# Attention with top-k, then two gated MLPs, on one core: the sign of the weights coded in a scaling, and probabilities normalised before the transpose

## The chip, the cores and the metric

The kernel runs on one core of a Trainium2 chip. The metric is the device time in microseconds (us) of one execution. A core has a matrix engine (TensorE, PE in the profile; its weight loads are the rows PEld), a vector engine (VectorE, DVE), an activation engine (ScalarE, ACT), a general engine (GpSimd, POOL) and an engine that issues transfers (SyncE, SP). Each engine takes its own instructions in the order in which the program lists them.

## The reference

```python
scores = (q @ k.T) / sqrt(64)                       # 4 batches, 8 heads, 576 queries, 576 keys
kth    = np.partition(scores, -32, axis=-1)[..., -32:-31]
scores = np.where(scores >= kth, scores, -1e9)      # the 32 largest of a row stay
attn   = exp(scores - max); attn /= attn.sum(-1) + 1e-9
x = attn @ v                                        # 2304 tokens of 512 numbers
h = x @ w_in;  x = (h * sigmoid(h)) @ w_out         # 512 -> 2048 -> 512
h = (x @ w1) * (x @ w2)                             # 512 -> 1024
out = (h @ w3) @ w_out2                             # 1024 -> 1024 -> 512
```

The weights `w_in`, `w_out`, `w1`, `w2`, `w3` and `w_out2` (`w4` in the kernel) reach the core as 64-bit floating-point numbers, two 32-bit words for each, while q, k and v are 32-bit. The kernel has to make 32-bit numbers of the weights on the chip.

## The kernel before, in words

The 2304 tokens are cut into six blocks of 384 (three tiles of 128 queries). For each block there is an attention part (8 heads, 24 tiles of queries) and an MLP part. While the MLP of block j runs, the attention of block j+1 runs beside it; the attention of block 0 runs beside the conversion of `w3` and `w4` and their product (the "fold"). Almost every product in the MLPs is made of three passes over numbers that are split into a high and a low part.

**Attention of a tile.** PE makes the scores (L415, L416), ACT copies them out (L419), DVE finds the 32 largest in four passes of `max` (L446) with three of `match_replace` between them (L450). ACT masks and exponentiates (L466, L472), DVE takes the reciprocal of the row sum (`rc`, L481, L482), and `norm` (L484) applies it. PE then transposes 128 x 128 pieces of the probabilities (`tr` in `plan_av`), ACT copies these out (L564), and PE multiplies them with V (L584).

**Native blocks.** Blocks 0 and 1 (`NATIVE`) multiply with V in full 32-bit precision, without a split. In them `norm` does not touch the probabilities `e`: it scales the identity with `rc` into a diagonal `dg` (128 x 128), on ACT for the first four pairs of tiles (L496), on GpSimd after that (L498), and PE multiplies `e` with `dg` (L553), which transposes and normalises at once. Such a matmul of 32-bit numbers stands in the profile as two instructions, so the 240 of the program are x480. In blocks 2 to 5 GpSimd normalises `e` itself (128 x 640, L498), and PE transposes it with the identity (L556, L558), one instruction for each piece.

**Conversion of a piece of weights** (512 columns of 128 rows, 72 pieces: 24 in the fold, 48 for the other four matrices). `convert_load` fetches both words of each number. `convert_scale` scales the high word, read as a float, by 2^-112 into a tile `t`, which moves its exponent to where the 32-bit one belongs, and turns the low word into the bits that are missing (ACT, L140, with a bias from the tile `low`). `convert_bits` shifts `t` left by 3 and ORs the low bits in (DVE, L150). The shift loses the sign, and there are two ways to give it back. For even pieces outside the fold (24) ACT scales (L136) and a second DVE pass ORs the sign bit in (L153). For the other 48 GpSimd scales (L138), ACT makes a sign of +1 or -1 (L143) and GpSimd multiplies with it (L156). For the 48 pieces outside the fold the number is then split into a high part (ACT, L201) and a low part (GpSimd, L202) and written to memory, from where the later blocks read it. These 48 conversions run beside the last part of block 0's attention and beside the first MLP.

**What sets the order.** Attention work is put at ticks (`plan`), and the steps of an MLP, of the fold and of the conversion are spread over the ticks (`Spread`). The tile framework then orders the instructions of all engines by its own estimate of times, so a change in one instruction can move others far from it.

Of the kernel before, what the change touches and what calls it, by code (L numbers as in the profile page):

```python
# [8 lines left out]
FP32 = mybir.dt.float32  # L9
FP32R = mybir.dt.float32r  # L10
U32 = mybir.dt.uint32
I32 = mybir.dt.int32
ACTF = mybir.ActivationFunctionType
ALU = mybir.AluOpType
# [4 lines left out]
SHIFT = 2.0 ** -112  # L19
BLOCKS = [3, 3, 3, 3, 3, 3]  # L20
# [8 lines left out]
NORM_ACT = lambda n: n < 4  # L29
BELOW = 1.0e34  # L30
SLOT = 7
NATIVE = lambda j: j < 2
SCALE_ACT = lambda n, fold: not fold and n % 2 == 0
SIGN_BITS = lambda n, fold: not fold and n % 2 == 0
# [18 lines left out]
def attention_moe_moe2_kernel(  # L53
# [13 lines left out]
    nc = tc.nc  # L67
    B, H, D2, S = qT.shape
# [10 lines left out]
    scale = 1.0 / float(D) ** 0.5  # L79
# [10 lines left out]
    pt_p = ctx.enter_context(tc.tile_pool(name="pt", bufs=2))  # L90
# [25 lines left out]
    n_conv = [0]  # L116

# [9 lines left out]
    def convert_scale(r, fold):  # L130
        n = n_conv[0]
        n_conv[0] += 1
        t = raw_p.tile([128, 512], FP32, tag="t", bufs=TB, name="t")
        h = r[:, :, 1].bitcast(FP32)
        if SCALE_ACT(n, fold):
            nc.scalar.activation(out=t, in_=h, func=ACTF.Copy, scale=SHIFT)  # L136
        else:
            nc.gpsimd.tensor_scalar(t, h, SHIFT, 1.0, op0=ALU.mult, op1=ALU.mult)  # L138

        nc.scalar.activation(out=r[:, :, 0].bitcast(I32), in_=r[:, :, 0], func=ACTF.Identity,  # L140
                             bias=low, scale=2.0 ** -29 * (1.0 - 2.0 ** -16))
        if not SIGN_BITS(n, fold):
            nc.scalar.activation(out=h, in_=h, func=ACTF.Sign)  # L143
        return t, SIGN_BITS(n, fold)

    def convert_bits(r, t_):
        t, bits = t_
        w = raw_p.tile([128, 512], FP32, tag="w", bufs=WB, name="w")
        wb, tb = w.bitcast(U32), t.bitcast(U32)
        nc.vector.scalar_tensor_tensor(out=wb, in0=tb, scalar=3, in1=r[:, :, 0],  # L150
                                       op0=ALU.logical_shift_left, op1=ALU.bitwise_or)
        if bits:
            nc.vector.scalar_tensor_tensor(out=wb, in0=r[:, :, 1], scalar=0x80000000, in1=wb,  # L153
                                           op0=ALU.bitwise_and, op1=ALU.bitwise_or)
        else:
            nc.gpsimd.tensor_tensor(out=w, in0=w, in1=r[:, :, 1].bitcast(FP32), op=ALU.mult)  # L156
        return w
# [120 lines left out]
    blocks = []  # L278
# [149 lines left out]
    def plan_topk(n, base):  # L428
        pr = pairs[n]
        m = len(pr)  # L430
        st = {}
# [52 lines left out]
        def norm(i):  # L484
            j, h, t = pr[i]
            hd = heads[j, h]
            e = st["e"][i]

            if NATIVE(j):
                if "d" not in hd:  # L490
                    hd["d"] = pt_p.tile([128, blocks[j][1]], FP32, tag="pl", bufs=3, name="dg")
                x, p = ident, hd["d"][:, t * 128:(t + 1) * 128]
            else:
                x = p = e
            if NORM_ACT(n):
                nc.scalar.activation(out=p, in_=x, func=ACTF.Copy, scale=st["rc"][:, i:i + 1])  # L496
            else:
                nc.gpsimd.tensor_scalar(p, x, st["rc"][:, i:i + 1], 1.0, op0=ALU.mult, op1=ALU.mult)  # L498
            hd["p"][t] = e
            tiles.pop(n, None)  # L500
# [20 lines left out]
    def plan_av(j, h):  # L521
# [12 lines left out]
        def begin():  # L534
            st["p"] = heads[j, h]["p"]
            st["d"] = heads[j, h].get("d")
# [7 lines left out]
        for kc in range(KC):  # L544
            u = {}

            def tr(u=u, kc=kc):
                u["ps"] = ps = bank("pt")
                for i in range(BLOCKS[j]):
                    p = st["p"][i]  # L550
                    if native:
                        kn = REM if kc == NFULL else 128
                        nc.tensor.matmul(ps[0:kn, i * 128:(i + 1) * 128], lhsT=p[:, kc * 128:kc * 128 + kn],  # L553
                                         rhs=st["d"][:, i * 128:(i + 1) * 128], start=True, stop=True)
# [346 lines left out]
```

## Time and profile before

| | us |
|---|---|
| three runs | 1194.24, 1195.57 (median), 1199.98 |
| profiled execution, its time | 1194.58 |
| its span (first to last instruction) | 1192.3 |
| MLP of block 0: first L655 to last L776 | 193.5 to 418.2 |
| last L776 of blocks 1 to 4 | 583.6, 746.8, 915.6, 1071.1 |

Times in the profile count from the start of the span. A row of a group of instructions reads: line, engine, operation, out<-in with shapes, count | busy us, mean ns of one | idle time of the engine just before them, and who ended it.

### The profile page before, as it was taken

The numbers are of one execution on the slowest core, as the hardware profiler recorded it, in microseconds if no ns is written. First come the engines' busy times: TensorE is split into PE (matmuls) and PEld (weight loads), VectorE is DVE, ScalarE is ACT, GpSimd is POOL, SyncE is SP. The second block draws the span as 40 slices with busy tenths as digits, with TensorE's granted clock in tenths as the row PEclk, the third lists the DMA queues.
The fourth block names the chain that finished last, engine by engine and source line by source line (L and its number), as shares of the span: only waits on it lengthen the run. The fifth ranks groups of instructions, "written<-read, shape, count | busy, mean of one in ns | idle before, by whom it ended". The sixth has DMA issues, their size and how long they took to land.

```text
span 1192.3 us, 19809 instructions
## 1 busy us (share of the span) xinstructions
PE 1117.7 (94%) x6216; PEld 989.3 (83%) x6216; DVE 933.7 (78%) x2136; ACT 860.6 (72%) x1931; POOL 760.5 (64%) x768
## 2 busy tenths in 40 slices
PE   4889959899889999999999999999999999999998
PEld 2445536788778899989899999999898999999997
DVE  6998899999999898988889897987789988701100
ACT  6786888798897587887778877877868778642221
POOL 5665583798987266686687866767755767542231
PEclk8899978999999999999999999999999999999999
DMA  9963484788979377757678776898766775538740
GB/s 296 296 212 111 144 303 162 242 283 322 344 271 338 109 230 249 226 186 231 216 226 279 234 245 206 294 314 274 253 205 212 235 241 171 187 113 281 244 166 26
DMA packets 127880, 273.54 MB, mean 229 GB/s; under 512 B 40480, under 2 KB 65056, under 8 KB 127776
## 3 DMA queue, kind: packets, MB, share of 16 engines
q1 hardware_dynamic: 119712, 245.02, 62.4%
q10 hardware_dynamic: 8064, 27.27, 5.9%
q8 instruction: 49, 0.80, 0.3%
q14 instruction: 55, 0.45, 0.1%
HBM read 216.14 MB, written 56.10 MB: 228 GB/s over the span
## 4 chain that ended last, share of the span: by engine, by line
PE 60%; ACT 6%; DVE 5%; issue 1%; POOL 1%; DMA 1%; SPq 0%; ACTq 0%; DVEq 0%
PE bank L656 13%; PE bank L657 13%; PE bank L655 13%; PE bank L776 8%; PE bank L593 4%; PE bank L556 3%; PE bank L415 2%; DVE top L446 2%; PE bank L416 2%; DVE wk L450 2%; DVE w L150 1%; ACT e L466 1%; PE bank L558 1%; ACT e L472 1%; PE bank L584 1%
## 5 line engine op out<-in xcount | busy, mean ns | idle before, releaser
L446 DVE MAX8 top<-wk 128x8 f32<-128x576 f32 x432 | 319.7, 752 | 3.7
L670 POOL TENSOR_TENSOR gl<-gf,gh 128x384 fp32r<-128x384 f32 x144 | 149.3, 1038 | 147.5 <-ACT gh L669 140.6
L450 DVE MATCH_REPLACE8 wk<-top,wk 128x576 f32<-128x576 f32 x288 | 213.3, 742 | 0.0
L574 POOL TENSOR_TENSOR pl<-pf,ph 128x384 fp32r<-128x384 f32 x128 | 129.7, 1020 | 66.3 <-ACT ph L572 57.6
L419 ACT ACTIVATE st<-bank 128x288 f32<-128x288 f32 (+1 forms) x320 | 127.7, 415 | 41.6 <-PE bank L416 39.1
L446 DVE MAX8 top<-st 128x8 f32<-128x576 f32 x144 | 107.6, 751 | 34.0 <-ACT st L419 33.7
L656 PE MATMUL bank<-gl,wt 128*128 128x384 f32 x384 | 131.6, 343 | 2.0 <-POOL gl L670 1.7
L655 PE MATMUL bank<-x2h,wt 128*128 128x384 f32 x384 | 131.6, 345 | 1.9 <-ACT x2h L714 1.4
L655 PE MATMUL bank<-xh,wt 128*128 128x384 f32 x384 | 130.4, 342 | 2.4 <-ACT pn L564 0.9
L656 PE MATMUL bank<-x2l,wt 128*128 128x384 f32 x384 | 130.2, 339 | 2.2 <-POOL x2l L715 1.9
L656 PE MATMUL bank<-xl,wt 128*128 128x384 f32 x384 | 129.5, 337 | 0.2 <-POOL xl L615 0.2
L657 PE MATMUL bank<-xh,wt 128*128 128x384 f32 x384 | 129.3, 337 | 0.0
L657 PE MATMUL bank<-x2h,wt 128*128 128x384 f32 x384 | 129.2, 337 | 0.0
L657 PE MATMUL bank<-gh,wt 128*128 128x384 f32 x384 | 128.8, 336 | 0.0
L466 ACT ACTIVATE e<-st,nt 128x576 f32<-128x576 f32 x144 | 105.3, 777 | 15.3 <-DVE nt L458 15.2
L415 PE MATMUL bank<-kk,qs 128*128 128x288 f32 x320 | 104.3, 338 | 12.8 <-ACT pn L564 6.8
L472 ACT ACTIVATE e<-e,nb 128x576 f32<-128x576 f32 x144 | 111.8, 779 | 1.7 <-DVE top L446 1.5
L669 ACT CAST gh<-gf 128x384 fp32r<-128x384 f32 x144 | 74.3, 518 | 52.2 <-DVE gf L764 33.6
L697 DVE SCALAR_TENSOR_TENSOR gf<-th,bank 128x384 f32<-128x384 f32 x96 | 52.1, 546 | 76.1 <-ACT th L692 73.6
L450 DVE MATCH_REPLACE8 wk<-top,st 128x576 f32<-128x576 f32 x144 | 106.6, 742 | 0.0
L571 ACT COPY pf<-bank 128x384 f32<-128x384 f32 (+1 forms) x160 | 77.6, 485 | 29.4 <-PE bank L556 22.2
L498 POOL TENSOR_SCALAR e<-e,rc 128x640 f32<-128x640 f32 x96 | 76.1, 808 | 31.3 <-DVE rc L482 26.6
(93 smaller groups left out, 2992.5 us busy)
## 6 DMA issues: line engine op xcount, KB each, us to landing
wt<-scr SPq DMA_DIRECT2D x240, 512.0 KB, 4.3
scr<-wt ACTq DMA_DIRECT2D x48, 512.0 KB, 4.9
k<-kk SPq DMA_DIRECT2D x32, 576.0 KB, 5.0
kk<-k SPq DMA_DIRECT2D x32, 576.0 KB, 5.5
raw<-in_w_dram SPq DMA_DIRECT2D x24, 512.0 KB, 5.4
kr<-in_kT_dram SPq DMA_DIRECT2D x32, 288.0 KB, 5.2
raw<-in_w3T_dram SPq DMA_DIRECT2D x16, 512.0 KB, 5.3
raw<-in_w_in_dram SPq DMA_DIRECT2D x16, 512.0 KB, 5.5
```

What stands on the lines that cost most here:

```text
L415: nc.tensor.matmul(ps[:, 0:HS], lhsT=q_, rhs=kk[:, 0, cs], start=True, stop=False)
L419: nc.scalar.activation(out=tiles[n][r0:r1, m, cs], in_=ps[r0:r1, 0:HS], func=ACTF.Copy, scale=scale)
L446: nc.vector.max(out=st["top"][:, i, r * 8:r * 8 + 8], in_=st["s" if r == 0 else "wk"][:, i])
L450: nc.vector.match_replace(out=st["wk"][:, i], in_to_replace=st["top"][:, i, r * 8:r * 8 + 8], in_values=st["s" if r == 0 else "wk"][:, i], ...
L466: nc.scalar.activation(out=e[:, 0:S], in_=st["s"][:, i], func=ACTF.Prelu, bias=st["nt"][:, i:i + 1], alpha=BELOW)
L472: nc.scalar.activation(out=e, in_=e, func=ACTF.Exp, bias=st["nb"][:, i:i + 1], accum_out=st["sm"][:, i, 0:1])
L574: nc.gpsimd.tensor_sub(out=pl[f], in0=pf[f], in1=ph[f])
L655: nc.tensor.matmul(ps, lhsT=wh, rhs=rh, start=first, stop=False)
L656: nc.tensor.matmul(ps, lhsT=wh, rhs=rl, start=False, stop=False)
L657: nc.tensor.matmul(ps, lhsT=wl, rhs=rh, start=False, stop=last)
L670: nc.gpsimd.tensor_sub(out=u["l"], in0=full, in1=u["h"])
L776: nc.tensor.matmul(oacc[t], lhsT=a[:, ts], rhs=b[:, i, :], start=(i == 0 and x == 0), stop=(i == NI - 1 and x == 2))
```

## The change

The conversion has one form for all 72 pieces. ACT scales the high word with a Prelu: positive numbers by 2^-112, negative ones by 2^-112 times 2^32, so a negative number's exponent is larger by 32. GpSimd then clamps the upper 16 bits of each result, as a signed 16-bit integer, from below at -28672, in place; after DVE's shift by 3 the bit that has been coded arrives as the sign bit. The second DVE pass, the ACT sign and the GpSimd product are gone, and so is the GpSimd scaling. In the native blocks `norm` now multiplies `e` (128 x 576) with `rc` on GpSimd for all tiles, and `tr` transposes with the identity; `dg` and the ACT form of `norm` are gone.

```diff
+SIGN = 2.0 ** 32
+FLOOR = -28672
-NORM_ACT = lambda n: n < 4
-SCALE_ACT = lambda n, fold: not fold and n % 2 == 0
-SIGN_BITS = lambda n, fold: not fold and n % 2 == 0
...
         t = raw_p.tile([128, 512], FP32, tag="t", bufs=TB, name="t")
-        h = r[:, :, 1].bitcast(FP32)
-        if SCALE_ACT(n, fold):
-            nc.scalar.activation(out=t, in_=h, func=ACTF.Copy, scale=SHIFT)
-        else:
-            nc.gpsimd.tensor_scalar(t, h, SHIFT, 1.0, op0=ALU.mult, op1=ALU.mult)
-
+        nc.scalar.activation(out=t, in_=r[:, :, 1].bitcast(FP32), func=ACTF.Prelu, scale=SHIFT, alpha=SIGN)
         nc.scalar.activation(out=r[:, :, 0].bitcast(I32), in_=r[:, :, 0], func=ACTF.Identity,
                              bias=low, scale=2.0 ** -29 * (1.0 - 2.0 ** -16))
-        if not SIGN_BITS(n, fold):
-            nc.scalar.activation(out=h, in_=h, func=ACTF.Sign)
-        return t, SIGN_BITS(n, fold)
+        top = t.bitcast(I16).rearrange("p (f t) -> p f t", t=2)[:, :, 1]
+        nc.gpsimd.tensor_scalar(top, top, 32767, FLOOR, op0=ALU.min, op1=ALU.max)
+        return t
...
-        nc.vector.scalar_tensor_tensor(out=wb, in0=tb, scalar=3, in1=r[:, :, 0],
+        nc.vector.scalar_tensor_tensor(out=w.bitcast(U32), in0=t.bitcast(U32), scalar=3, in1=r[:, :, 0],
                                        op0=ALU.logical_shift_left, op1=ALU.bitwise_or)
-        if bits:
-            nc.vector.scalar_tensor_tensor(out=wb, in0=r[:, :, 1], scalar=0x80000000, in1=wb,
-                                           op0=ALU.bitwise_and, op1=ALU.bitwise_or)
-        else:
-            nc.gpsimd.tensor_tensor(out=w, in0=w, in1=r[:, :, 1].bitcast(FP32), op=ALU.mult)
...
-            if NATIVE(j):
-                if "d" not in hd:
-                    hd["d"] = pt_p.tile([128, blocks[j][1]], FP32, tag="pl", bufs=3, name="dg")
-                x, p = ident, hd["d"][:, t * 128:(t + 1) * 128]
-            else:
-                x = p = e
-            if NORM_ACT(n):
-                nc.scalar.activation(out=p, in_=x, func=ACTF.Copy, scale=st["rc"][:, i:i + 1])
-            else:
-                nc.gpsimd.tensor_scalar(p, x, st["rc"][:, i:i + 1], 1.0, op0=ALU.mult, op1=ALU.mult)
+            p = e[:, 0:S] if NATIVE(j) else e
+            nc.gpsimd.tensor_scalar(p, p, st["rc"][:, i:i + 1], 1.0, op0=ALU.mult, op1=ALU.mult)
...
-                        nc.tensor.matmul(ps[0:kn, i * 128:(i + 1) * 128], lhsT=p[:, kc * 128:kc * 128 + kn],
-                                         rhs=st["d"][:, i * 128:(i + 1) * 128], start=True, stop=True)
+                        nc.tensor.transpose(ps[0:kn, i * 128:(i + 1) * 128], p[:, kc * 128:kc * 128 + kn], ident)
```

In the order of the built program the lines of the changed kernel are numbered anew: its Prelu is L127, its clamp L131, its only DVE pass L136, its `norm` L471, its native transpose L525; `max` is L427, `match_replace` L431, the reciprocal L463, the gate of the MLP L668.

On DVE, in the first MLP, before the change (L150 and L153 are the conversion, L446 and L450 the search for the 32 largest, L697 the gate of the MLP):

```order
L450 MATCH_REPLACE wk<-top,wk 128x576
L150 SCALAR_TENSOR_TENSOR w<-t,raw 128x512
L446 MAX top<-wk 128x8
L482 RECIPROCAL rc<-rc 128x2
L446 MAX top<-wk 128x8
L153 SCALAR_TENSOR_TENSOR w<-raw,w 128x512
L450 MATCH_REPLACE wk<-top,wk 128x576
L150 SCALAR_TENSOR_TENSOR w<-t,raw 128x512
L697 SCALAR_TENSOR_TENSOR gf<-th,bank_91 128x384
```

and around the same gate after it:

```order
L136 SCALAR_TENSOR_TENSOR w<-t,raw 128x512
L427 MAX top<-st 128x8
L431 MATCH_REPLACE wk<-top,st 128x576
L435 TENSOR_REDUCE top<-top 128x2
L427 MAX top<-wk 128x8
L668 SCALAR_TENSOR_TENSOR gf<-th,bank_94 128x384
L431 MATCH_REPLACE wk<-top,wk 128x576
L136 SCALAR_TENSOR_TENSOR w<-t,raw 128x512
L427 MAX top<-wk 128x8
L431 MATCH_REPLACE wk<-top,wk 128x576
L427 MAX top<-wk 128x8
L668 SCALAR_TENSOR_TENSOR gf<-th,bank_91 128x384
```

The second pass is gone, and two to four instructions of the search stand between one conversion and the next.

On GpSimd, in the same part of the program, before (L138 and L156 are the conversion, L202 the split of a piece, L338 and L498 belong to the attention):

```order
L156 TENSOR_TENSOR w<-w,raw 128x512
L138 TENSOR_SCALAR t<-raw 128x512
L202 TENSOR_TENSOR wt<-w,wt 128x512
L338 TENSOR_TENSOR qs<-qr,qs 64x384
L138 TENSOR_SCALAR t<-raw 128x512
L156 TENSOR_TENSOR w<-w,raw 128x512
L202 TENSOR_TENSOR wt<-w,wt 128x512
L498 TENSOR_SCALAR dg<-ident,rc 128x128 x2
L202 TENSOR_TENSOR wt<-w,wt 128x512
```

and after (L131 is the clamp, L183 the split, L471 the normalising of `e`, L319 the split of a query tile, L641 the split of a gated tile):

```order
L131 TENSOR_SCALAR t<-t 128x512
L183 TENSOR_TENSOR wt<-w,wt 128x512
L319 TENSOR_TENSOR qs<-qr,qs 64x384
L471 TENSOR_SCALAR e<-e,rc 128x576 x2
L131 TENSOR_SCALAR t<-t 128x512
L183 TENSOR_TENSOR wt<-w,wt 128x512
L641 TENSOR_TENSOR gl<-gf,gh 128x384
L131 TENSOR_SCALAR t<-t 128x512
L183 TENSOR_TENSOR wt<-w,wt 128x512
```

Every piece now has one GpSimd instruction ahead of DVE's pass, where half of the pieces outside the fold had none and the other half one ahead of it and one behind it.

On PE, in the first MLP, before (L553 is the product with the diagonal, one row for two instructions of the profile):

```order
L584 MATMUL bank_91<-pn,vn 64x192 x2
L553 MATMUL bank_90<-dg,e 128x128 x3
L553 MATMUL bank_92<-dg,e 128x128 x3
L415 MATMUL bank_91<-kk,qs 128x288
L416 MATMUL bank_91<-kk,qs 128x288
L655 MATMUL bank_94<-xh,wt 128x384
```

and after (L555 is L584 of before, L396 is L415, L626 is L655):

```order
L555 MATMUL bank_91<-pn,vn 64x192 x2
L525 MATMUL bank_90<-ident,e 128x128 x3
L626 MATMUL bank_94<-xh,wt 128x384
L627 MATMUL bank_94<-xl,wt 128x384
L628 MATMUL bank_94<-xh,wt 128x384
```

The three products with a diagonal became three transposes with the identity, in about the same place.

## Rows read from the trace of the kernel before

The columns of rows 1, 6, 10 and 11, which are windows of the trace, are: from:to, length in us; busy us with the count of instructions, in rows 1 and 11 for PE, PEld, DVE, ACT and POOL in this order, in the others for the engines that the line of text names; then the granted share of PE's clock, the busy share of the transfer engines and their GB/s.

**Rows 1.** Busy time of the engines in five stretches of the span:

```profile
0.00:180.00 180.00, 140.48 (x510) 78.59 (x511) 157.28 (x343) 137.27 (x286) 114.89 (x117) 0.89 0.70 228
180.00:240.00 60.00, 53.41 (x280) 42.35 (x278) 56.98 (x127) 48.09 (x105) 32.34 (x33) 0.92 0.60 201
240.00:360.00 120.00, 110.43 (x635) 95.25 (x635) 112.96 (x213) 109.37 (x229) 108.19 (x96) 1.00 0.88 307
360.00:420.00 60.00, 59.58 (x339) 51.18 (x338) 51.57 (x111) 38.59 (x85) 31.88 (x33) 1.00 0.65 218
420.00:1192.30 772.30, 753.85 (x4460) 721.88 (x4458) 554.88 (x1345) 527.24 (x1230) 473.18 (x490) 1.00 0.66 221
```

**Rows 2.** Chain that ended last, shares by line: 240 to 360 us, then 360 to 420:

```profile
by line: DVE top L446 10.3%; DVE wk L450 8.2%; DVE w L150 7.4%; issue 5.0%; DMA vn<-in_v_dram 3.3%; DVE w L153 3.0%; POOL wt L202 2.6%; POOL gl L670 2.0%; ACT raw L140 1.2%; ACT t L136 1.1%; ACT e L466 1.1%; ACT gh L669 1.0%; POOL t L138 0.
...
by line: PE bank L776 21.0%; PE bank L655 14.0%; PE bank L584 13.6%; PE bank L553 12.2%; PE bank L656 12.2%; PE bank L657 11.9%; PE bank L415 4.8%; PE bank L416 3.7%; DVE w L150 3.0%; POOL wt L202 2.8%; DVE w L153 1.8%; DVE gf L764 0.9%; is
```

**Rows 3.** Groups by line, the conversion's instructions over the whole span:

```profile
L150 DVE SCALAR_TENSOR_TENSOR w<-t,raw 128x512 uint32<-128x512 uint32 x72 | 72.8, 1020 | 24.9 <-ACT raw L140 9.8 <-issue 6.5 <-POOL wt L202 4.1
...
L202 POOL TENSOR_TENSOR wt<-w,wt 128x512 fp32r<-128x512 f32 x48 | 66.8, 1399 | 11.1 <-ACT wt L201 11.1
...
L156 POOL TENSOR_TENSOR w<-w,raw 128x512 f32<-128x512 f32 x48 | 65.5, 1365 | 28.1 <-DVE w L150 15.9 <-issue 5.7 <-ACT raw L143 3.8
...
L140 ACT ACTIVATE raw<-raw,low 128x512 int32<-128x512 uint32 x72 | 55.4, 771 | 19.8 <-DMA raw<-in_w3T_dram 5.3 <-DMA raw<-in_w_out_dram 4.2 <-DMA raw<-in_w_dram 4.1
...
L138 POOL TENSOR_SCALAR t<-raw 128x512 f32<-128x512 f32 x48 | 39.5, 823 | 10.9 <-DMA raw<-in_w_out_dram 5.4 <-DVE w L150 3.4 <-DMA raw<-in_w3T_dram 1.1
...
L143 ACT ACTIVATE raw<-raw 128x512 f32<-128x512 f32 x48 | 32.4, 678 | 8.0 <-POOL t L138 8.0
...
L153 DVE SCALAR_TENSOR_TENSOR w<-raw,w 128x512 uint32<-128x512 uint32 x24 | 26.4, 1102 | 0.1
...
L136 ACT ACTIVATE t<-raw 128x512 f32<-128x512 f32 x24 | 16.3, 679 | 3.0 <-DVE w L150 1.1 <-POOL wt L202 1.1 <-POOL w4l L249 0.8
```

**Rows 4.** The first DVE pass by itself, ns min/median/max:

```profile
L150 DVE SCALAR_TENSOR_TENSOR w<-t,raw x72: 665/788/1840, 8.0 to 375.1; 128x512 uint32<-128x512 uint32 x72
```

**Rows 5.** Timeline at 360 us: start, duration, engine, line:

```profile
360.24 1.31 POOL L156 TENSOR_TENSOR w<-w,raw 128x512 f32<-128x512 f32 x1
...
360.31 1.79 DVE L150 SCALAR_TENSOR_TENSOR w<-t,raw 128x512 uint32<-128x512 uint32 x1 [1.18 <-POOL wt L202]
```

**Rows 6.** Busy time of L153 alone, by stretch:

```profile
0.00:180.00 180.00, 5.75 (x5) 0.89 0.70 228
180.00:240.00 60.00, 3.13 (x3) 0.92 0.60 201
240.00:360.00 120.00, 14.76 (x14) 1.00 0.88 307
360.00:420.00 60.00, 2.80 (x2) 1.00 0.65 218
```

**Rows 7.** GpSimd in 240 to 360 us, groups by line:

```profile
L156 POOL TENSOR_TENSOR w<-w,raw 128x512 f32<-128x512 f32 x13 | 17.5, 1344 | 3.1 <-DVE w L150 1.8 <-ACT raw L140 1.3
...
L138 POOL TENSOR_SCALAR t<-raw 128x512 f32<-128x512 f32 x13 | 11.7, 898 | 3.2 <-DVE w L150 2.8 <-DMA raw<-in_w_out_dram 0.3
L498 POOL TENSOR_SCALAR dg<-ident,rc 128x128 f32<-128x128 f32 x14 | 7.3, 535 | 0.7 <-DVE rc L482 0.7
```

**Rows 8.** Groups by line: normalising in blocks 2 to 5:

```profile
L498 POOL TENSOR_SCALAR e<-e,rc 128x640 f32<-128x640 f32 x96 | 76.1, 808 | 31.3 <-DVE rc L482 26.6 <-ACT pf L571 2.3 <-PE bank L556 1.1
```

**Rows 9.** Chain pieces, start and us: products with a diagonal, transposes with the identity:

```profile
399.80 1.34 PE bank L553 x12
...
960.22 0.33 PE bank L556 x3
```

**Rows 10.** Busy time of L553 alone on PE and PEld, 360 to 420 us:

```profile
360.00:420.00 60.00, 9.31 (x66) 8.19 (x66) 1.00 0.65 218
```

**Rows 11.** Busy time of the engines in 30 us of block 0's attention:

```profile
150.00:180.00 30.00, 15.33 (x63) 10.37 (x62) 29.96 (x62) 25.51 (x54) 23.58 (x22) 0.70 0.87 306
```

More of the change, by code (lines that the diff above doesn't have):

```diff
@@ L12 @@
 I32 = mybir.dt.int32
+I16 = mybir.dt.int16
 ACTF = mybir.ActivationFunctionType
@@ L115, in attention_moe_moe2_kernel @@
     sums = w4_p.tile([128, 4, 2, 2], FP32, name="sums")
-    n_conv = [0]
     def convert_load(ap):
@@ L130, in convert_scale, with convert_bits @@
     def convert_scale(r, fold):
-        n = n_conv[0]
-        n_conv[0] += 1
         t = raw_p.tile([128, 512], FP32, tag="t", bufs=TB, name="t")
-        h = r[:, :, 1].bitcast(FP32)
-        if SCALE_ACT(n, fold):
-            nc.scalar.activation(out=t, in_=h, func=ACTF.Copy, scale=SHIFT)
-        else:
-            nc.gpsimd.tensor_scalar(t, h, SHIFT, 1.0, op0=ALU.mult, op1=ALU.mult)
+        nc.scalar.activation(out=t, in_=r[:, :, 1].bitcast(FP32), func=ACTF.Prelu, scale=SHIFT, alpha=SIGN)
         nc.scalar.activation(out=r[:, :, 0].bitcast(I32), in_=r[:, :, 0], func=ACTF.Identity,
                              bias=low, scale=2.0 ** -29 * (1.0 - 2.0 ** -16))
-        if not SIGN_BITS(n, fold):
-            nc.scalar.activation(out=h, in_=h, func=ACTF.Sign)
-        return t, SIGN_BITS(n, fold)
-    def convert_bits(r, t_):
-        t, bits = t_
+        top = t.bitcast(I16).rearrange("p (f t) -> p f t", t=2)[:, :, 1]
+        nc.gpsimd.tensor_scalar(top, top, 32767, FLOOR, op0=ALU.min, op1=ALU.max)
+        return t
+    def convert_bits(r, t):
         w = raw_p.tile([128, 512], FP32, tag="w", bufs=WB, name="w")
-        wb, tb = w.bitcast(U32), t.bitcast(U32)
-        nc.vector.scalar_tensor_tensor(out=wb, in0=tb, scalar=3, in1=r[:, :, 0],
+        nc.vector.scalar_tensor_tensor(out=w.bitcast(U32), in0=t.bitcast(U32), scalar=3, in1=r[:, :, 0],
                                        op0=ALU.logical_shift_left, op1=ALU.bitwise_or)
-        if bits:
-            nc.vector.scalar_tensor_tensor(out=wb, in0=r[:, :, 1], scalar=0x80000000, in1=wb,
-                                           op0=ALU.bitwise_and, op1=ALU.bitwise_or)
-        else:
-            nc.gpsimd.tensor_tensor(out=w, in0=w, in1=r[:, :, 1].bitcast(FP32), op=ALU.mult)
         return w
@@ L535, in begin @@
             st["p"] = heads[j, h]["p"]
-            st["d"] = heads[j, h].get("d")
             st["v"] = heads[j, h]["v"]
```

## Prediction

> **What bounds the kernel now.** I read the busy time of the engines by stretch first. After 420 us PE is busy 753.9 of 772.3 us, and no line of the change runs there except the normalising of blocks 2 to 5, which stays as it is [rows 1]; so whatever the change is worth, it is worth before 420 us. There the picture differs by stretch. From 0 to 180 us (fold and attention of block 0) DVE is the fullest, 157.3 of 180, and most of its gaps lie at the start, where the loads arrive. From 180 to 240 it has 57.0 of 60. From 240 to 360, where the conversions are densest, four engines are nearly full at once: DVE 113.0, PE 110.4, ACT 109.4 and POOL 108.2 of 120. From 360 to 420 it is PE, 59.6 of 60 [rows 1]. The chain of waits agrees where it reaches: it goes back to about 300 us, is led by DVE's lines until 360, L153 among them, and by PE's lines after that [rows 2].
>
> **What the change removes from DVE.** The second pass, L153, is 24 instructions of 1102 ns, 26.4 us [rows 3]. By stretch it is 5.75, 3.13, 14.76 and 2.80 us [rows 6]. The pass that stays, L150, takes 1020 ns on average, 72.8 us in all [rows 3], but 665 ns at its shortest [rows 4], so 72.8 - 72 x 0.665 = 24.9 us of it are something else. The timeline shows what: an L150 that starts while GpSimd is in its two-input product L156 lasts 1.79 us, until some time after that product has ended [rows 5]. The change takes L156 away, 65.5 us [rows 3] of the 287.3 us for which POOL is busy before 420 us (114.9 + 32.3 + 108.2 + 31.9) [rows 1], that is 23%. I take 23% of the 24.9 us, 5.7 us, as DVE's gain by this; the bounds are 0 (the new clamp holds DVE up as much) and 24.9 us (L150 always at its shortest). By the count of conversions in the stretches it is about 2.6, 0.6, 2.2 and 0.3 us.
>
> **GpSimd.** Out go L138 and L156, 39.5 + 65.5 = 105.0 us [rows 3]. In come 72 clamps. The trace has no 16-bit instruction, so I bound one from both sides: the diagonal of the dense stretch, a quarter of the columns, takes 535 ns [rows 7], and the dearest GpSimd instruction of 512 columns is the two-input L202, 1399 ns [rows 3]. I take L138, 823 ns [rows 3], because it too has one input with two operations on 512 columns and a stride: 59.3 us. The normalising of the native blocks becomes 128 x 576; the row at 128 x 640 has 808 ns [rows 8], which I take, against 535 ns for the diagonal. For 240 to 360 us alone: out 17.5 + 11.7 us [rows 7], in 27 clamps (13 L138 plus the 14 even pieces) of 823 ns, 22.2 us, and 14 x (808 - 535) ns = 3.8 us more of normalising: 108.2 - 29.2 + 22.2 + 3.8 = 105.0 us. So GpSimd does not become the bound by this price.
>
> **ACT.** Out go 24 scalings of 679 ns and 48 signs of 678 ns [rows 3], in come 72 Prelus. Each has the strided input of those and no bias tile, so I take 679 ns: nothing won and nothing lost. The upper bound is L140 on the same 512 columns, which does have a bias tile, 771 ns [rows 3]: 72 x 92 ns = 6.6 us more, a third of it in the dense stretch. (The Trainium skill, "ScalarE: Activation LUTs", What ACT_TABLE_LOAD costs, gives 186 ns + 0.833 ns a column without pointer operands, an estimate of 613 ns at 512 columns and 93 ns more for a bias pointer. By that the 72 Prelus would cost 44 us, 5 us less than the row makes them; the 93 ns agree with the 92 between the rows of L140 and L143.)
>
> **PE.** A 128 x 128 piece of the native blocks costs two products now, 12 of which take 1.34 us in the chain, so 0.22 us a piece; three transposes take 0.33 us, 0.11 us a piece [rows 9]. That is 0.11 us less for 240 pieces, 26 us of PE, but it counts only where PE is the bound: from 360 to 420 us there are 66 such instructions [rows 10], 33 pieces, 3.7 us. The wait of PE for `dg` becomes one for `e`, 0.3 us later by the longer normalising, while PE has gaps there.
>
> **The sum by stretch.** 0 to 180: DVE is the bound, its 5.75 + 2.6 us pass whole, -8.4. 180 to 240: 3.1 + 0.6, -3.7. 240 to 360: DVE loses 14.8 + 2.2 = 17 us and falls to 96 of 120, but ACT keeps its 109.4 us and becomes the fullest. Packed without a gap it would let the stretch shrink by 10.6 us; at the 94% that DVE reaches today (113.0 of 120), 109.4 / 0.94 = 116.4, by 3.6 us. I take the middle, -7.1. 360 to 420: the 3.7 us of PE, and DVE's relief does not pass. Together -22.9 us. The sum is against the profiled execution: 1194.58 - 22.9 = 1171.7 us; the median of the three runs, 1195.57, lies 1.0 us above that execution, so I say 1172.5 us. In the changed order nothing has taken the place of L153 on DVE; the search follows at once.
>
> **The rivals.**
> A, *everything of DVE's relief passes.* ACT's fullness in the dense stretch is only a matter of place, since it has 48.1 of 60 before and 38.6 of 60 after it [rows 1]; if attention work slides over, the 17 us pass whole and the sum is -8.4 - 3.7 - 17.0 - 3.7 = -32.8, 1163 us. For it: DVE leads the chain there, ACT does not [rows 2]. Against: both follow the same order of program.
> B, *GpSimd becomes the bound.* At 1399 ns a clamp the dense stretch holds 27 x 1.40 = 37.8 us of clamps and POOL comes to 108.2 - 29.2 + 37.8 + 3.8 = 120.6 of 120: it wins nothing there, and the sum is -15.8, 1180 us. For it: no row of the trace has 16-bit halves in place. Against: one input, not two.
> C, *the clamp stands in front of DVE's pass* (the slower side). Until now only the pieces that GpSimd scales wait for GpSimd before L150, and that scaling needs only the loaded data; now each of the 72 passes waits for ACT and then for GpSimd, and behind it on DVE wait the `max` and `match_replace` of the search. The idle time before L150 is 24.9 us in all today [rows 3], 0.35 us each. If the wait grew by half an L202 in front of the clamp, 0.70 us, DVE would lose 72 x 0.70 = 50 us: 1172.5 + 50 = 1223 us. It decides from 23 / 72 = 0.32 us a pass. Against it: two to four instructions of the search now stand between two passes, and a piece's clamp is issued a step ahead of its pass.
> D, *PE falls back to half clock in the attention of block 0.* From 150 to 180 us PE is busy 15.3 of 30 us and the granted clock is 0.70, between its levels of 1.2 and 2.4 GHz, while DVE is full (29.96) [rows 11]. If it stayed at the lower level through 0 to 180 us, PE's 140.5 us at 0.89 [rows 1] would be 140.5 x 0.89 / 0.5 = 250 us, less 26 us for the 120 pieces of block 0 (0.11 us each, twice as long at that level): 224 us, 44 over the stretch, and DVE's 8.4 us would be lost too: 1172.5 + 44 + 8.4 = 1225 us. (The Trainium skill, "TensorE: Matmul & The Clock Gate", Part 4: PE-mode transpose, says that the full clock does not engage for transposes; after 420 us, where blocks 2 to 5 transpose so among dense products, the row has 1.00.)
> E, *no change.* If ACT and the order, not DVE, hold the first 240 us and the dense stretch, only the last stretch's 3.7 us are left: 1195.6 - 3.7 = 1192 us.
>
> **How the numbers follow.** A measurement of this kernel tells about 0.5%, 6 us, from no change, so "faster" is below 1189.6 us. My forecast (1167 to 1178) has 0.50, A 0.18, B 0.16, E 0.08, C 0.06, D 0.02. Faster is forecast, A and B: 0.84; same E, 0.08; slower C and D, 0.08. The range of 8 in 10 leaves out C, D and the half of E above, and of A the part beyond DVE's 5.7 us of shorter passes (with all 24.9 us the time would be near 1150): 1157 to 1189 us.
>
> **What would show it.** Right: L136 x72 at 900 to 950 ns and nothing in L153's place; DVE's search of block 1 ends earlier, so that the first L655 stands some 8 us before 193.5 us and the last L776 of block 0 some 23 us before 418.2; the later blocks keep their distances of 155.5 to 168.8 us; the clamp near 0.8 us, the Prelu near 0.68 us; ACT above 93% in the dense stretch. Wrong: idle time in front of L136 put down to L131 (C), POOL full in the dense stretch (B), the clock below 0.89 in the first 180 us (D), or an ACT that is full earlier than the dense stretch (E).

## The result, and the profile after

The changed kernel takes 1203.3 us (median of 6 runs, 1199.64 to 1211.7) against 1195.63 us for the kernel before measured beside it (6 runs, 1194.24 to 1199.98): a ratio of 1.0059 [1.0035, 1.0083], so it is 0.6% slower, clear of the scatter of the runs, where 1172.5 us was forecast. The profiled execution is the longest of the six, 1211.7 us with a span of 1209.6 us: what is read from its trace adds up to 17.3 us against the trace of before, more than the 7.7 us between the medians, and which part of it the shorter executions lack is not known.

The busy time of the engines in the five stretches, columns as in [rows 1]:

```profile
0.00:180.00 180.00, 131.63 (x409) 65.62 (x409) 154.69 (x345) 134.35 (x280) 92.55 (x100) 0.88 0.67 221
180.00:240.00 60.00, 52.20 (x248) 38.74 (x247) 55.65 (x126) 49.84 (x107) 38.86 (x38) 0.91 0.67 223
240.00:360.00 120.00, 95.48 (x481) 80.56 (x479) 85.29 (x179) 95.47 (x199) 87.98 (x81) 0.89 0.81 270
360.00:420.00 60.00, 58.52 (x318) 49.65 (x318) 47.54 (x104) 42.44 (x91) 38.15 (x37) 1.00 0.77 257
420.00:1209.60 789.60, 769.83 (x4525) 736.57 (x4524) 560.61 (x1362) 535.01 (x1250) 479.14 (x496) 0.99 0.66 218
```

The dense stretch, 240 to 360 us, is where the two kernels part. In [rows 1] all four engines have 108 to 113 us of work in it. Now PE, DVE, ACT and POOL have 85 to 95 us: not one took the place of another, they all wait.

The instructions themselves came out close to their prices. Groups by line, to be set against [rows 3] and, for the last line, [rows 8]:

```profile
L136 DVE SCALAR_TENSOR_TENSOR w<-t,raw 128x512 uint32<-128x512 uint32 x72 | 64.8, 903 | 21.6 <-POOL t L131 15.3 <-POOL wt L183 4.5 <-issue 1.8
L131 POOL TENSOR_SCALAR t<-t 128x512 int16<-128x512 int16 x72 | 60.3, 837 | 70.2 <-ACT t L127 60.4 <-DMA kr<-in_kT_dram 2.6 <-PE bank L397 2.2
L128 ACT ACTIVATE raw<-raw,low 128x512 int32<-128x512 uint32 x72 | 55.4, 770 | 31.8 <-DMA raw<-in_w_dram 10.2 <-DMA raw<-in_w3T_dram 8.4 <-DMA raw<-in_w_in_dram 6.6
L127 ACT ACTIVATE t<-raw 128x512 f32<-128x512 f32 x72 | 48.8, 678 | 20.2 <-DVE w L136 13.5 <-DMA vn<-in_v_dram 3.3 <-DMA raw<-in_w_dram 3.1
...
L471 POOL TENSOR_SCALAR e<-e,rc 128x576 f32<-128x576 f32 x48 | 39.6, 835 | 19.1 <-DVE rc L463 6.7 <-ACT pn L535 4.6 <-ACT a L729 3.5
```

So the pass on DVE (L150 before, L136 now) is shorter, L153 is gone, the clamp L131 costs 837 ns and the Prelu L127 678 ns. But the idle time before L128 is 31.8 us, where L140 had 19.8 [rows 3], and loads of `raw` end most of it.

The waits inside the MLP of block 0 (engine, line, what it waited for: us in total, times, longest) show what hangs on that. Before, 193 to 418 us:

```profile
DVE top L446 <- ACT st L419: 5.0, 2, 3.0
```

After, 190 to 434 us:

```profile
DVE top L427 <- ACT st L400: 25.3, 11, 8.8
...
ACT raw L128 <- DMA raw<-in_w_dram: 9.8, 4, 4.5
...
ACT raw L128 <- DMA raw<-in_w_in_dram: 5.0, 2, 4.1
```

DVE's search waits five times as long for ACT's copies of the scores (L419 before, L400 now). The timeline of after around 343 us (start, duration, engine, line, in brackets the wait) shows how the two belong together; a q behind an engine is its queue:

```profile
335.68 4.65 SPq L122 DMA_DIRECT2D raw<-in_w_dram  x3
...
338.26 0.61 ACT L182 CAST wt<-w 128x512 fp32r<-128x512 f32 x1
...
343.36 0.74 ACT L128 ACTIVATE raw<-raw,low 128x512 int32<-128x512 uint32 x1 [4.50 <-DMA raw<-in_w_dram]
...
344.74 0.76 POOL L131 TENSOR_SCALAR t<-t 128x512 int16<-128x512 int16 x1 [3.69 <-ACT t L127]
...
345.98 0.69 PE L626 MATMUL bank<-x2h,wt 128*128 128x384 f32 x1 [7.78 <-ACT x2h L685]
346.47 0.44 PE L396 MATMUL bank<-kk,qs 128*128 128x288 f32 x1
...
348.29 0.45 ACT L400 ACTIVATE st<-bank 128x288 f32<-128x288 f32 x1
...
348.77 0.76 DVE L427 MAX8 top<-st 128x8 f32<-128x576 f32 x1 [8.84 <-ACT st L400]
```

ACT waits 4.50 us for a load in front of L128, and runs nothing else in that time. L685, for which PE waits 7.78 us, stands behind it, the scores (L396) come behind that product on PE, and L400, for which DVE waits 8.84 us, copies those scores. Only the 3.4 us to 343.36 of DVE's 8.84 lie in ACT's wait itself; in the rest ACT and PE do what had been held back. The chain of waits in the dense stretch has loads of `raw` at its head, which the chain of [rows 2] has nowhere in the part that it reaches, from 298 us on:

```profile
by line: DMA raw<-in_w_dram 11.5%; DMA raw<-in_w_in_dram 7.5%; DVE wk L431 7.0%; PE bank L628 6.9%; PE bank L627 6.7%; DVE top L427 6.7%; PE bank L626 5.7%; PE bank L555 5.0%; issue 4.9%; DMA raw<-in_w_out_dram 4.7%; DVE w L136 4.6%; ACT t 
```

### The profile page after: what moved, and what is told of

The parts are those of the page before. It is cut to its first block, busy times and chain, and to the rows that moved or that the text cites. A ratio compares the mean times of both kernels' runs of the same rounds, so it can differ in the third digit from the quotient of the medians.

```text
span 1209.6 us, 19235 instructions
## 1 busy us (share of the span) xinstructions
PE 1107.7 (92%) x5976; PEld 971.1 (80%) x5976; DVE 903.8 (75%) x2112; ACT 857.1 (71%) x1923; POOL 736.7 (61%) x752
## 4 chain that ended last, share of the span: by engine, by line
PE 65%; ACT 8%; DVE 6%; DMA 3%; issue 2%; POOL 1%; ACTq 0%; DVEq 0%; POOLq 0%; SPq 0%
PE bank L627 14%; PE bank L628 14%; PE bank L626 14%; PE bank L747 8%; PE bank L564 4%; PE bank L527 3%; PE bank L396 3%; DVE top L427 2%; PE bank L555 2%; PE bank L397 2%; DVE wk L431 2%; ACT e L447 1%; ACT e L453 1%; DMA raw<-in_w_dram 1%; ACT st L400 1%
## 5 line engine op out<-in xcount | busy, mean ns | idle before, releaser
L427 DVE MAX8 top<-wk 128x8 f32<-128x576 f32 x432 | 320.1, 752 | 4.3
L641 POOL TENSOR_TENSOR gl<-gf,gh 128x384 fp32r<-128x384 f32 x144 | 148.6, 1034 | 142.3 <-ACT gh L640 140.5
L431 DVE MATCH_REPLACE8 wk<-top,wk 128x576 f32<-128x576 f32 x288 | 213.4, 742 | 0.0
L400 ACT ACTIVATE st<-bank 128x288 f32<-128x288 f32 (+1 forms) x320 | 128.0, 414 | 47.0 <-PE bank L397 45.5
L427 DVE MAX8 top<-st 128x8 f32<-128x576 f32 x144 | 107.7, 752 | 63.2 <-ACT st L400 62.4
L471 POOL TENSOR_SCALAR e<-e,rc 128x640 f32<-128x640 f32 (+1 forms) x144 | 115.8, 817 | 52.9 <-DVE rc L463 28.0
L626 PE MATMUL bank<-x2h,wt 128*128 128x384 f32 x384 | 132.3, 347 | 9.5 <-ACT x2h L685 8.9
L626 PE MATMUL bank<-xh,wt 128*128 128x384 f32 x384 | 130.8, 344 | 8.0 <-DVE gf L668 2.9
L627 PE MATMUL bank<-gl,wt 128*128 128x384 f32 x384 | 134.4, 350 | 1.1 <-POOL gl L641 0.8
L628 PE MATMUL bank<-gh,wt 128*128 128x384 f32 x384 | 132.2, 344 | 0.0
L396 PE MATMUL bank<-kk,qs 128*128 128x288 f32 x320 | 107.0, 346 | 24.8 <-ACT pn L535 10.4
L668 DVE SCALAR_TENSOR_TENSOR gf<-th,bank 128x384 f32<-128x384 f32 x96 | 52.2, 546 | 83.3 <-ACT th L663 81.8
L431 DVE MATCH_REPLACE8 wk<-top,st 128x576 f32<-128x576 f32 x144 | 106.7, 742 | 0.0
L131 POOL TENSOR_SCALAR t<-t 128x512 int16<-128x512 int16 x72 | 60.3, 837 | 70.2 <-ACT t L127 60.4
```

The costliest lines, as they stand in the source:

```text
L396: nc.tensor.matmul(ps[:, 0:HS], lhsT=q_, rhs=kk[:, 0, cs], start=True, stop=False)
L400: nc.scalar.activation(out=tiles[n][r0:r1, m, cs], in_=ps[r0:r1, 0:HS], func=ACTF.Copy, scale=scale)
L427: nc.vector.max(out=st["top"][:, i, r * 8:r * 8 + 8], in_=st["s" if r == 0 else "wk"][:, i])
L431: nc.vector.match_replace(out=st["wk"][:, i], in_to_replace=st["top"][:, i, r * 8:r * 8 + 8], in_values=st["s" if r == 0 else "wk"][:, i], ...
L471: nc.gpsimd.tensor_scalar(p, p, st["rc"][:, i:i + 1], 1.0, op0=ALU.mult, op1=ALU.mult)
L626: nc.tensor.matmul(ps, lhsT=wh, rhs=rh, start=first, stop=False)
```

## The experiments

All ratios are to a kernel before on the same chip (medians 1195.6 to 1197.6 us). "Start" is the start of the first product in the MLP of block 0, "end" that of the last (L655 and L776 in the kernel before), both from the span's start in the profiled execution; "rest" is from there to the last such product of block 5. The last two columns are idle time between start and end, summed over the rows of the waits.

| kernel | median us | ratio to before | start | end | rest | ACT for loads of raw | DVE for ACT |
|---|---|---|---|---|---|---|---|
| before | 1195.6 |  | 193.5 | 418.2 | 767.8 | 1.3 | 8.5 |
| after | 1203.3 | 1.0059 [1.0035, 1.0083] | 190.7 | 434.3 | 769.0 | 15.9 | 42.5 |
| e1, conversion alone | 1194.2 | 0.9975 [0.9958, 0.9991] | 189.1 | 427.2 | 762.2 | 18.3 | 46.7 |
| e2, native part alone | 1192.5 | 0.9969 [0.995, 0.9987] | 177.7 | 412.7 | 769.8 | 1.9 | 11.5 |
| e3, t in place | 1232.1 | 1.0305 [1.0276, 1.0334] | 198.9 | 456.5 | 765.4 | 24.2 | 67.0 |
| e4, before without L153 | 1190.7 | 0.9951 [0.9934, 0.9968] | 190.0 | 418.8 | 765.4 | 3.6 | 15.7 |
| e5, after, smaller rings | 1196.4 | 0.9992 [0.9973, 1.001] | 185.8 | 422.4 | 765.6 | 14.9 | 41.4 |
| e6, e5 with 3 t buffers | 1209.9 | 1.0119 [1.0086, 1.0152] | 187.2 | 434.8 | 767.7 | 19.2 | 56.3 |
| e7, e5 with 5 raw buffers | 1205.5 | 1.0066 [1.0039, 1.0092] | 193.4 | 425.5 | 774.3 | 18.6 | 43.9 |
| e8, after without loads | 1187.2 | 0.9922 [0.9895, 0.995] | 185.9 | 414.7 | 760.8 | 0 | 34.5 |
| e9, before without loads | 1198.9 | 1.0004 [0.9985, 1.0024] | 193.1 | 418.6 | 771.7 | 0 | 8.9 |
| e10, before, smaller rings | 1193.9 | 0.9973 [0.9955, 0.9991] | 197.1 | 426.8 | 764.2 | 3.0 | 15.2 |
| e11, before, other order | 1264.6 | 1.0557 [1.0518, 1.0595] | 183.8 | 455.8 | 801.5 | 0.3 | 35.1 |
| e12, after, other order | 1260.2 | 1.0517 [1.0477, 1.0557] | 178.0 | 450.2 | 800.3 | 0.2 | 13.5 |
| e13, after, steps behind copy | 1186.8 | 0.9909 [0.9881, 0.9938] | 183.6 | 417.7 | 762.4 | 0 | 37.0 |
| e14, before, steps behind copy | 1205.0 | 1.0064 [1.0041, 1.0086] | 193.5 | 430.0 | 767.1 | 0.5 | 14.9 |
| e15, e2, smaller rings | 1185.4 | 0.9907 [0.988, 0.9934] | 178.1 | 413.3 | 767.2 | 8.2 | 9.9 |
| e16, e13, smaller rings | 1196.2 | 0.9977 [0.9954, 1.0] | 184.7 | 417.1 | 771.0 | 1.3 | 30.6 |

### Which half, and was DVE the bound: e1 to e4

e1 takes only the conversion, e2 only the native part, of the change. e3 lets the Prelu write in place into `raw`, so that the ring of `t` (a ring is the set of buffers that successive tiles use in turn) is no longer waited for:

```diff
-        t = raw_p.tile([128, 512], FP32, tag="t", bufs=TB, name="t")
+        t = r[:, :, 1].bitcast(FP32)
```

e4 is the kernel before without its second DVE pass; the sign of 24 pieces is left out:

```diff
-        if bits:
-            nc.vector.scalar_tensor_tensor(out=wb, in0=r[:, :, 1], scalar=0x80000000, in1=wb,
-                                           op0=ALU.bitwise_and, op1=ALU.bitwise_or)
-        else:
+        if not bits:
```

> The changed kernel with the old native part: blocks 0 and 1 scale the identity into dg (on ACT for the first four pairs) and multiply with it; only the new conversion of the weights stays. Theory 1 (the loss sits in the conversion: each piece now goes ACT, GpSimd, DVE and back to ACT over two buffers t and four raw buffers, and ACT, which works in order, stands at the head of it): about as slow as the changed kernel, 1200 to 1206 us, MLP of block 0 again near 244 us against 225 before, ACT idle in front of L127 and L128 by some 20 us in that stretch. Theory 2 (the loss sits in the native blocks: the longer normalising on GpSimd and the transposes): clearly faster than before, near 1175 us. Theory 3 (the framework shuffles the order of the first 420 us with any edit, and the time scatters by it): anywhere in 1185 to 1210.

> The kernel before with the new native part alone: normalising of e on GpSimd and transposes with the identity in blocks 0 and 1, old conversion. Theory 1: PE loses about 26 us of work, of which 4 to 8 us count: 1187 to 1192 us. Theory 2: slower than before, 1200 us or more, with PE idle in front of the transposes. Theory 3: anywhere in 1185 to 1210.

> The changed kernel, but the Prelu writes its result over the high word in the raw buffer, the clamp works there, and DVE reads both words from there: no piece waits for one of the two t buffers any more, all the work stays. Theory 1 in the form that the two t buffers are the narrow place: the 14 us for which ACT waits in front of the Prelu for DVE's pass go, and MLP of block 0 comes back to 225 us or less, 1180 to 1190 us in all. Theory 1 in the form that the raw loads are it: ACT still waits for the loads by 15 us or more in MLP 0 and the time stays within 1198 to 1206 us. Theory 2: no change, 1203 us.

> The kernel before without the second DVE pass L153: the 24 even pieces outside the fold lose their sign, everything else stays. It shows what DVE's 26.4 us are worth by themselves, without clamp, Prelu or native part. If DVE is the bound as the prediction had it: 1195.6 - 19 to 26, 1170 to 1177 us. If ACT, the loads or the order hold the dense stretch: 1185 to 1196 us. Theory 3: 1185 to 1210.

Each half alone is a little faster than before, both together slower: the effects do not add, which effects that sit in a sum of work would. e1 waits for loads and for ACT as much as after does (18.3 and 46.7 us) and yet is no slower than before, against the 1200 to 1206 us that theory 1 gave it: such waits alone do not make the kernel slow. e4 answers the question of the bound. Its windows:

```profile
0.00:180.00 180.00, 141.97 (x513) 78.69 (x514) 155.71 (x341) 137.29 (x287) 111.25 (x116) 0.89 0.70 223
180.00:240.00 60.00, 52.10 (x284) 40.78 (x283) 53.85 (x125) 50.38 (x109) 35.15 (x36) 0.98 0.67 224
240.00:360.00 120.00, 110.95 (x630) 96.91 (x629) 99.20 (x199) 107.62 (x227) 103.31 (x99) 0.97 0.90 308
```

DVE has 13.8 us less to do in the dense stretch than in [rows 1], PE gets through the same work (110.95 against 110.43 us), and block 0 ends at 418.8 instead of 418.2 us. The time freed in this stretch turned into idle time of DVE. The whole is 0.5% shorter than before, 5.9 us for 26.4 us of work, and the framework has ordered this kernel anew too. e3 has no ring of `t` and came out slower than any of its theories said: its loads are waited for most (24.2 us) and its clamp is dearer (last section); which of the two made it slow is not shown.

### More buffers: e5 to e7

A third `t` or a fifth `raw` buffer fits only beside smaller rings in attention, so e5 is the control, with one buffer less in two of them: `EB = 6`, `XB = 5`. This is what is called a neutral edit below: it takes no work away. e6 adds `TB = 3`, e7 `RB = 5`.

> The changed kernel with two rings of the attention cut to make room (e from 7 to 6 tiles, xh and xl from 6 to 5): the control for the next two. Theory 1 says nothing of it: 1200 to 1215 us, no better than the changed kernel. Theory 3 (scatter of the order by any edit): anywhere in 1190 to 1215.

> The control with a third buffer for t. Theory 1a (the two t buffers are the narrow place: the Prelu of a piece waits on ACT for DVE's pass of the piece before the last): the wait of ACT in front of the Prelu goes, the MLP of block 0 falls from about 244 to 230 us or less, and the time is 12 us or more below the control. Theory 1b (the raw loads are the narrow place: four raw buffers, and ACT is now the first reader of every piece, so it stands waiting for the load with the scores behind it): within 4 us of the control, ACT still waiting some 16 us for loads in the MLP of block 0.

> The control with a fifth raw buffer. Theory 1b: a load is issued one piece earlier, some 5 us, ACT's 16 us of waiting for loads in the MLP of block 0 falls under 5 us, and the time is 12 us or more below the control. Theory 1a: within 4 us of the control.

Both theories of a short ring fell: against e5, where one of them had to gain 12 us, a buffer more costs 13 and 9 us. The control itself gave 7 us by having less. The same work scatters by 13 us among after, e5, e6 and e7, which differ in their rings and in the order that the framework makes for them.

### Loads left out: e8 and e9

Of the 48 pieces converted beside attention only the first 4 are loaded, the others convert the same bytes again:

```diff
-            conv_st[k] = convert_load(halves[k])
+            conv_st[k] = kept[k % 4] = convert_load(halves[k]) if k < 4 else kept[k % 4]
```

> The changed kernel, but outside the fold only the first four pieces are loaded; the other 44 are made from the same four raw tiles again, so the weights are wrong, no load stands in the way of ACT, and 23 MB of reads go. Theory 1b: the MLP of block 0 falls to 215 us or less and the time to 1180 us or less. Theory 1a (the t buffers): the two t buffers still bind and the time stays above 1192 us.

> The kernel before, in which only the first 4 of the 48 weight pieces are loaded and the later ones convert the same bytes again (their weights are wrong); no instruction of a calculating engine is taken out. In the changed kernel the same cut was worth 16 us, 15 of them in the MLP of block 0 (243.6 to 228.8 us). Theory 3a (only the changed conversion is held up by loads, because there ScalarE, which also feeds VectorE with scores, is the first reader of every piece): the MLP of block 0 of the kernel before stays at 222 to 226 us, since ScalarE waits only 1.3 us for loads there, and the whole stays within 1190 to 1197 us. Rival (the loads cost both kernels alike, through the buffers or the DMA queues): the MLP of block 0 falls by 10 us or more, to under 215 us, and the whole to under 1184 us.

The same cut is worth 16 us in the changed kernel, between what the two theories gave it, and nothing in the kernel before (1.0004). Before and after have as many loads, and as long ones (5.6 us from issue to landing, the mean of the last 40 pieces): what changed is who waits for them. My reading by then, that it matters which engine reads a piece first, was too simple, as e12 shows next.

### Another order: e10 to e12

e10 is the neutral edit of e5 on the kernel before. e11 and e12 let the framework order the program without its simulation of the timeline, which follows the written order more closely.

> The kernel before with EB 7 to 6 and XB 6 to 5, the rings that made the changed kernel 7 us faster (1196.4 against 1203.3 us) though they only take buffers away. Theory 3b (each edit makes the framework order the program anew, and kernels of the same work scatter by some 7 us either way): anything from 1188 to 1205 us, the difference lying in the MLP of block 0. Rival (smaller rings are good of themselves, in both kernels): 1187 to 1191 us. Rival (the kernel before was at a favourable order, which any edit loses): above 1200 us.

> The kernel before, ordered by the framework without its simulation of the timeline: the same work in another order on each engine. Gives the kernel before a second order to stand against the same of the changed kernel. Theory 3b (order scatter): differs from 1196 us by more than 5 us, either way. If the order hardly matters: 1194 to 1198 us.

> The changed kernel, ordered by the framework without its simulation of the timeline, to be set beside the kernel before in that order. Theory 3a (ScalarE as first reader costs the changed conversion 15 to 24 us of waiting for loads in the MLP of block 0 in any order): this kernel is slower than the kernel before in the same order by 3 to 12 us, and ScalarE waits over 10 us for loads there. Theory 3b alone (the loss is an accident of the order): it is faster than the kernel before in the same order, by the 5 to 20 us that the work taken out is worth.

The order alone is worth 5.6%, ten times the effect that is to be explained, and the neutral edit of e10 is worth as much as each half of the change. In the other order the change gives 1260.2 / 1264.6 = 0.997, and ACT waits 0.2 us for loads although it is the first reader of every piece there too: it takes a piece up 13.3 us after its landing, against 1.5 us in after (means of the last 40 pieces). So the load waits do not come from the first reader as such, but from the place in ACT's queue that the framework gives to a piece's steps.

### The order held: e13 to e16

In e13 ACT's two steps on piece k are kept behind its copy of piece k-2 by an edge of order in the same queue. No buffer, instruction or load differs; the order in which the steps are written changes with it:

```diff
+        a = k - 4
+        if 0 <= a < NH:
+            w = conv_st.pop(a)
+            t = new_piece(0, a)
+            c = nc.scalar.copy(out=t[:, 0], in_=w)
+            nc.gpsimd.tensor_sub(out=t[:, 1], in0=w, in1=t[:, 0])
+            copied[:] = [getattr(c, "ins", c)]
         a = k - 2
         if 0 <= a < NH:
-            conv_st[a] = (conv_st[a], convert_scale(conv_st[a], False))
+            with (tc.issue_after(copied[0]) if copied else nullcontext()):
+                conv_st[a] = (conv_st[a], convert_scale(conv_st[a], False))
```

e14 is the same edit of the kernel before, e15 is e2 with the smaller rings, e16 is e13 with the smaller rings.

> The changed kernel in which ScalarE's two steps on piece k stand behind its copy of piece k-2 in its queue (an edge of order, no wait added), so that ScalarE takes a piece up only when the OR two pieces earlier is over; its load, issued when the OR four pieces earlier is over, has then had about two paces (9 us) for its 5.6 us. Same instructions, buffers and loads. Theory 3c (ScalarE, put ahead in the queue to a load that is late, holds back the scores' evictions for which VectorE and with it the next OR wait): ScalarE's waiting for loads in the MLP of block 0 falls from 16 to under 4 us, that MLP from 243.6 to 226 to 234 us, the whole to 1185 to 1194 us. Rival (scatter alone; load waits are a symptom): the load waits fall and the MLP of block 0 stays above 238 us, the whole at 1196 us or more.

> The kernel before with the same edges of order. There ScalarE waits only 1.3 us for loads, so theory 3c has nothing to gain: 1192 to 1204 us. If such an order is good of itself, whatever the conversion: under 1190 us.

> The conversion of before, the changed probabilities and transposes of the first two blocks, and the smaller rings EB 6 and XB 5. The two edits alone gave 0.9969 and 0.9973 of the kernel before. If the native part's gain of 3.7 us is its own (26 us of TensorE's work less in the blocks where it has waits) and outlasts another order: 1184 to 1194 us. Scatter alone: anything from 1188 to 1203 us, above 1194 us about as likely as below.

> The changed kernel with ScalarE's two steps behind the copy of piece k-2, and the smaller rings EB 6 and XB 5, which were worth -7 us in the changed kernel and -3.7 us in the kernel before. If the held order is the cause of e13's gain: 1180 to 1192 us, with under 4 us of ScalarE's waiting for loads in the MLP of block 0 and that MLP at 234 us or less. If e13 was a lucky order: back in the scatter of the changed kernels, 1196 to 1210 us.

e13's windows and its waits in the MLP of block 0 (183 to 417 us):

```profile
240.00:360.00 120.00, 101.30 (x510) 86.67 (x509) 90.09 (x188) 101.99 (x213) 94.55 (x89) 0.89 0.85 296
...
DVE top L430 <- ACT st L403: 18.4, 8, 4.8
```

The waits for loads are gone, the longest wait of the search for ACT fell from 8.8 to 4.8 us, and block 0 ends at 417.7 instead of 434.3 us; DVE's waits for ACT as a whole fell little, from 42.5 to 37.0 us. e16 keeps the load waits (1.3 us) and the end of block 0 (417.1 us) through a neutral edit, but not the time: beside e5, its control with the same rings, it ends block 0 5.3 us sooner, takes 5.4 us more for the rest, and comes to 1196.2 against 1196.4 us. The same edges make the kernel before slower (e14, 1.0 us above what was expected), so they are not good of themselves. By piece (mean of the last 40; each piece's load, L128 and L136, or L140 and L150 in before, matched in order): ACT took a piece up 3.2 us after its landing in before, 1.5 us in after, 8.5 us in e13; from L128 to the DVE pass it was 7.4, 13.8 and 6.2 us.

e15 shows that the native part alone keeps its gain under the smaller rings. Together with e5 it also gives a second measure of what the new conversion costs on top of the native part: from e15 to e5 the ratio grows by 0.0085, as from e2 to after by 0.0090, some 10 us each time. With the smaller rings the held order does not take this away: e16 lies 0.0070 above e15, though its load waits are gone.

Two more readings of these expectations. Of the 16.6 us by which e13 ends block 0 sooner only 9.5 lie in the MLP itself (243.6 to 234.1); the other 7.1 are an earlier start. And e16's whole time, 1196.2 us, is outside the 1180 to 1192 us of the held order and at the edge of what was said for a lucky order (1196 to 1210 us): its later blocks take 771.0 us, e13's 762.4 us. That rest lies between 760.8 and 774.3 us in all kernels ordered in the framework's usual way. e13 (1186.8) and e15 (1185.4) beat both kernels, but an edit as neutral as a ring size can take that away.

## Why the prediction was wrong

**From 0 to 360 us DVE is the bound, and what is taken from it passes.** This step failed; 19.2 of the 22.9 us rested on it. I read 113 of 120 us [rows 1] and a chain led by DVE's lines [rows 2] as a bound. e4 takes no work out but L153, and DVE's relief does not pass: L153 has 8.9 us before 240 us [rows 6], and the MLP of block 0 starts 3.5 us earlier; from there on nothing is won, and block 0 ends at 418.8 us, 0.6 us later than before. The new waits for loads in front of ACT's L128, 15.9 us in the MLP of block 0, stood in the sum at nothing. Four engines at 108 to 113 us of 120 that wait for one another in order look the same as one bound with three followers; only taking work away tells them apart.

**The sizes of the terms were right.** L136 came to 903 ns (900 to 950 said), shorter than L150 by 8.0 us in all (5.7 said); the clamp to 837 ns (823 said), the Prelu to 678 (679 said), the normalising of the native blocks to 835 (808 said). The Prelu's shortest is 642 ns, so the row of the trace was the better price than the estimate of 613 ns worked out from the Trainium skill, "ScalarE: Activation LUTs", What ACT_TABLE_LOAD costs. Three transposes take 0.33 us in the chain:

```profile
398.85 0.33 PE bank L525 x3
404.25 0.33 PE bank L525 x3
```

**0 to 240 us, -8.4 and -3.7.** Right in direction, wrong in size. The MLP of block 0 starts 2.8 us earlier in after, 8 us earlier was said; in after, e1 and e5 to e8 it starts at 185.8 to 193.4 us, in e3 at 198.9. The native part alone brings it to 177.7 (e2) and 178.1 (e15), where I gave it nothing; but in e2 the end of block 0 comes only 5.5 us earlier than before, so most of that start is lost again.

**240 to 360 us, -7.1.** The sign was wrong. I asked which engine would be fullest next, and ACT at "above 93%" was my sign of being right; it has 95.47 of 120, 80%. The question was what stands in the queues. Each piece's way became ACT, GpSimd, DVE, where before half of the pieces outside the fold had their scaling from GpSimd, and the framework's new order put ACT's L128 in front of copies of scores, and in front of loads that had not landed.

**360 to 420 us, -3.7.** Cannot be seen by itself, since the end of block 0 is late as a whole.

**The rivals.** A, all of DVE's relief, fell with the same step. C, new waits for a dearer hop, is nearest in kind, but its place was wrong: its sign is there, 15.3 us in front of L136 put down to L131, but the idle time in front of the DVE pass fell from 24.9 us [rows 3] to 21.6 instead of growing by 50. The new wait stands in front of the search and is for ACT, not for GpSimd. B fell (POOL 87.98 of 120, the clamp at 837 ns). D fell for the first stretch (0.88 against 0.89 [rows 1]), while the dense one fell from 1.00 to 0.89 as PE's busy time fell from 110.43 to 95.48 us; e13 has 0.89 there too and ends block 0 at 417.7 us, so this alone did not make the end late. E, ACT and the order instead of DVE as what holds the first 240 us and the dense stretch, was right about the order, but I took the order as fixed, and so it gave 1192 us.

**What stays open.** That the load waits lengthen the first MLP of the changed kernel is borne out by e8 and e13: without them its end comes at 414.7 and 417.7 us instead of 434.3, and the whole is 16 us shorter each time. That they are the cause of the 7.7 us is not shown: e1 has them and is not slower, e16 is rid of them and is no faster than e5, and 7 us is what a neutral edit moves (after to e5). Nor do they alone set the end of block 0. In the usual order, with under 4 us of them, it lies at 412.7 to 418.8 us in before, e2, e4, e8, e9, e13 and e16, whatever was taken from DVE, but at 426.8 us in e10 and 430.0 us in e14; e15 has 8.2 us of them and ends at 413.3 us. What holds the end there I did not find; in e13's chain of the dense stretch the loads of `kr`, which attention needs, now stand first:

```profile
by line: DMA kr<-in_kT_dram 14.6%; issue 7.5%; PE bank L629 5.9%; PE bank L558 5.4%; ACT raw L128 5.3%; ACT t L127 5.3%; DVE top L430 5.2%; PE bank L630 5.1%; DVE wk L434 5.0%; ACT wt L177 5.0%; DVE w L136 4.8%; PE bank L631 4.7%; ACT e L45
```

Nor is it shown why the framework takes up a piece earlier with the new conversion in all five kernels of the usual order that were looked at for it (1.2 to 1.7 us after its landing in after, e1, e5, e6 and e7).

## What to carry to other kernels

Where several engines are all nearly full and wait for each other in order, work taken from the fullest is worth nothing until a run without that work shows that it is; make that run first. Where a framework orders the program anew with every edit, look first at what each in-order queue now has in front of its waits for loads, and set a neutral edit beside the change before a difference under 1% is called the change's. Where an edge of order removes the wait, try it, and check the whole time under another neutral edit: here the wait stayed away and the gain did not.

## What was not expected of the hardware

The clamp's step in bytes went with its time. In `t` the 16-bit halves lie 4 bytes apart and the clamp takes 837 ns; in e3 they lie 8 bytes apart, in `raw`, for what it reads and what it writes, and it takes 1378 ns, from the groups by line of e3:

```profile
L131 POOL TENSOR_SCALAR raw<-raw 128x512 int16<-128x512 int16 x72 | 99.2, 1378 | 64.3 <-ACT raw L127 51.8 <-DVE top L427 6.6 <-PE bank L628 1.7
```

(The Trainium skill, "GPSIMD Engine Reference", Performance pitfalls for Q7 kernels, puts a price on reads whose step is above 8 bytes, for kernels written for GpSimd's cores; this instruction takes 541 ns more at 8 bytes already.) The step of the read alone is not the reason: L138 reads 32-bit words 8 bytes apart and writes them packed in 823 ns [rows 3]. Whether the write's step or the 16-bit type makes the difference no run shows. And a 16-bit operation in place on half-words, of which the kernel before has no row, costs what one of 32 bits does: 837 ns against L138's 823 [rows 3].
